# The opening of a spectral kernel: sine tables first with idle matmuls over the wait, and row statistics six rows ahead instead of eight

## The chip, the cores and the metric

The kernel runs on one core of a Trainium2 chip. The metric is the device time of one execution in microseconds, median over several executions. Every comparison below is with executions of the kernel before on the same chip in the same rounds.

## The reference, cut to what matters

The program computes a block with a spectral filter and a mixing layer over the sequence, and its gradients by `jax.vjp`.

```python
def _A_ref(x, w_r, w_i):              # x: 1 x 2048 x 448, bf16
    X = rfft2(x.astype(float32), axes=(-2, -1))
    X = X * (w_r + 1j * w_i)
    return irfft2(X, s=(2048, 448), axes=(-2, -1)).astype(bfloat16)

def _B_ref(x, w1, b1, w2, b2):
    h = layernorm(x)
    u = gelu(einsum("bsd,sf->bdf", h, w1) + b1)
    return (einsum("bdf,fs->bds", u, w2) + b2).transpose(0, 2, 1)

h  = x + _A_ref(layernorm(x), w_r, w_i)
h2 = h + _B_ref(layernorm(h), w1, b1, w2, b2)
# outputs: h2 and the gradients for grad_out with respect to x, w_r, w_i, w1, b1, w2, b2
# ... (inputs, random keys and helper names cut)
```

Only the start of it matters here. The 2048 rows of x are held as 16 "rows" of 128 partitions. Each needs its mean and deviation (the layer norm), and then enters the transform. Matrix multiplications of grad_out with w2 (a gradient of `_B_ref`) are independent of this, so the kernel uses them to fill TensorE between the row transforms.

## The kernel before

The Fourier transforms are matrix multiplications with sine tables that the kernel makes itself. For a row `t` of x, `scale_R` multiplies the table `Rm` by the row's reciprocal deviation (VectorE), `fold_prep` makes sums and differences of the two halves of two rows (VectorE), and `row_a` multiplies the two on TensorE. `row_b` follows four rows behind `row_a` with the second table, `csF`.

```python
def scale_R(t):
    v = Rs_ring.next()                                   # four buffers
    ve.tensor_scalar(out=v, in0=Rm[:], scalar1=rstd_x[:, t:t + 1], scalar2=None, op0=ALU.mult)
    return v

def newton_gp(v, y, sl):       # reciprocal deviations of two rows, ten dependent steps on GpSimd
    vi, yi = nt_i[:, 0, sl], y.bitcast(I32)
    a = nt_f[:, 0, sl]
    gp_.tensor_scalar(out=v, in0=v, scalar1=LN_EPS, scalar2=None, op0=ALU.add)
    gp_.tensor_scalar(out=yi, in0=v.bitcast(I32), scalar1=-0.5, scalar2=RSQRT_MAGIC, op0=ALU.mult, op1=ALU.add)
    for c0, c1 in RSQRT_STEPS:                           # two Newton steps
        gp_.tensor_tensor(out=a, in0=y, in1=y, op=ALU.mult)
        gp_.tensor_tensor(out=a, in0=a, in1=v, op=ALU.mult)
        gp_.tensor_scalar(out=a, in0=a, scalar1=c0, scalar2=c1, op0=ALU.mult, op1=ALU.add)
        gp_.tensor_tensor(out=y, in0=a, in1=y, op=ALU.mult)
```

The loop over the rows. `STATS[t]` lists the rows whose statistics VectorE takes in iteration `t`, `GROUPS[t]` the pair whose roots GpSimd then makes, and `fill(n)` issues n gradient matmuls.

```python
GROUPS = {0: (6, 8), 1: (8, 10), 3: (10, 12), 5: (12, 14), 7: (14, 16)}
STATS = {0: (6, 7), 1: (8, 9), **{t: (t + 8,) for t in range(2, 8)}}
# ...
for t in range(NT):                                      # NT = 16
    # ... (loads cut)
    if t + 1 < NT:
        row_a(t + 1, Rs.pop(t + 1))
    fill(FILL_A[t])
    if 1 <= t and t + 3 < NT:
        # ...
        Rs[t + 3] = scale_R(t + 3)
    row_b(t - 3)
    # ...
    if t % 2 and t < 12:
        fold_prep(xn, t // 2 + 2)
    for i in STATS.get(t, ()):
        ln_stats(xn, i, mvx)
    # ... (parts of the other sine tables cut)
    if t in GROUPS:
        a, b = GROUPS[t]
        newton_gp(mvx[:, a:b, 1], rstd_x[:, a:b], slice(a, b))
    # ...
    fill(FILL_B[t])
```

Copies of TensorE's results out of the tiles `ps_ff` and `ps_mm` may run on either VectorE or ScalarE.

Of the kernel before, what the change touches and what calls it, by code (L numbers as in the profile page):

```python
# [13 lines left out]
ALU = mybir.AluOpType  # L14
# [3 lines left out]
P = 128  # L18
# [83 lines left out]
class Ring:  # L102
# [7 lines left out]
    def next(self):  # L110
        v = self.views[self.i % len(self.views)]
        self.i += 1
        Ring.release(v)
        return v
# [8 lines left out]
def kernel(  # L123
# [20 lines left out]
    nc = tc.nc  # L144
# [3 lines left out]
    ve = Meter(nc.vector, load, 1)  # L148
# [13 lines left out]
    def cut(reg, off, *dims):  # L162
        n = int(np.prod(dims))
        v = reg[:, off:off + n]
        if len(dims) == 1:
            return v
        names = "abcd"[:len(dims)]
        return v.rearrange("p (" + " ".join(names) + ") -> p " + " ".join(names),
                           **{c: d for c, d in zip(names, dims)})
# [5 lines left out]
    def ps_ff(parts=P):  # L175
        return psum.tile([P, 512], F32, tag="ff", bufs=4, name="ps_ff")

    def ps_mm():
        return psum.tile([P, 512], F32, tag="mm", bufs=4, name="ps_mm")


    def evac(out, in_, scale=None):
        n = int(np.prod(in_.shape[1:]))
        if load[0] + sc.cost('copy', n, False) <= load[1] + ve.cost('tensor_copy', n, in_.dtype == BF16):
            if scale is None:
                sc.copy(out=out, in_=in_)
            else:
                sc.activation(out=out, in_=in_, func=ACT.Copy, scale=scale)
        elif scale is None:
            ve.tensor_copy(out=out, in_=in_)  # L190
        else:
            ve.tensor_scalar(out=out, in0=in_, scalar1=scale, scalar2=None, op0=ALU.mult)
# [24 lines left out]
    def mm(out, lhsT, rhs, start, stop):  # L217
        nc.tensor.matmul(out, lhsT=lhsT, rhs=rhs, start=start, stop=stop)  # L218
        clock[0] += int(np.prod(rhs.shape[1:])) / 2400.0
        run_due()  # L220
# [25 lines left out]
    csF = mem.tile([P, 2, 2, KW], BF16, name="csF")  # L246
    csI = mem.tile([P, 2, 2, D], BF16, name="csI")
    ident = mem.tile([P, P], BF16, name="ident")
# [6 lines left out]
    def col(n=1):  # L255
        i = _ci[0]
        _ci[0] += n
        assert _ci[0] <= 64
        return cols[:, i:i + n]

    xn = cut(rA, 0, NT, D)
# [26 lines left out]
    x_pt = A_x[0].rearrange("(p t) d -> p t d", t=NT)  # L288
# [3 lines left out]
    def load_w2T():  # L292
        j = w2T_ring.i
        if j == NFB:
            return
        wT = w2T_ring.next()
        nc.sync.dma_start_transpose(out=wT, in_=B_w2[j * P:(j + 1) * P, :].rearrange("f (t c) -> f t c", c=P))  # L297
        w2Ts.append(wT)
# [7 lines left out]
    def load_go(q):  # L306
        nc.sync.dma_start(out=go_tp[:, 4 * q:4 * q + 4, :], in_=go_tp_d[:, 4 * q:4 * q + 4, :])

    nc.sync.dma_start(out=xn[:, 0:2, :], in_=x_pt[:, 0:2, :])
    load_w2T()  # L310
    load_go(0)
    nc.sync.dma_start(out=xn[:, 2:4, :], in_=x_pt[:, 2:4, :])
    load_go(1)
    load_x(1)
    load_go(2)
# [13 lines left out]
    def ftmp(off, *dims):  # L329
        n = int(np.prod(dims))  # L330
        v = tf[:, off:off + n]
        if len(dims) == 1:
            return v
        names = "abcd"[:len(dims)]
        return v.rearrange("p (" + " ".join(names) + ") -> p " + " ".join(names),
                           **{c: d for c, d in zip(names, dims)})
# [11 lines left out]
    sc.activation(out=warm, in_=warm, func=ACT.Sin)  # L348
    nc.vector.memset(rAT[:, 0:512], 0.0)
    idle = ps_mm()  # L350
    for _ in range(12):
        nc.tensor.matmul(idle[:, 0:D], lhsT=rAT[:, 0:P], rhs=rAT[:, 0:D], start=True, stop=True)

    pcol = col()
# [4 lines left out]
    krow = ftmp(0, D)  # L359
# [169 lines left out]
    def gen_inv_cols(ch):  # L529
        e, en = col(), col()  # L530
        inv_cols[ch] = (e, en)
        gp_.memset(e, 2.0)
        if ch == 0:
            gp_.memset(e[0:1, :], 1.0)
        else:
            gp_.tensor_scalar(out=e, in0=pcolb, scalar1=112.0, scalar2=None, op0=ALU.is_equal)
            gp_.tensor_scalar(out=e, in0=e, scalar1=-1.0, scalar2=2.0, op0=ALU.mult, op1=ALU.add)
            gp_.memset(e[0:1, :], 0.0)
        gp_.tensor_scalar(out=en, in0=e, scalar1=-1.0, scalar2=None, op0=ALU.mult)
        gp_.tensor_scalar(out=halves[:, ch:ch + 1], in0=e, scalar1=-0.5, scalar2=1.5, op0=ALU.mult, op1=ALU.add)  # L540
# [82 lines left out]
    def scale_R(t):  # L623
        v = Rs_ring.next()
        ve.tensor_scalar(out=v, in0=Rm[:], scalar1=rstd_x[:, t:t + 1], scalar2=None, op0=ALU.mult)
        return v
# [5 lines left out]
    def fold_prep(src, t2):  # L632
        ft = fold_ring.next()
        s0 = 2 * t2
        fv = ft[:, 0:2 * D].rearrange("p (s w j) -> p s w j", s=2, w=2)
        a = src[:, s0:s0 + 2, 0:D // 2]
        r = src[:, s0:s0 + 2, D - 1:D // 2 - 1:-1]
        ve.tensor_tensor(out=fv[:, :, 0, :], in0=a, in1=r, op=ALU.add)
        ve.tensor_tensor(out=fv[:, :, 1, :], in0=a, in1=r, op=ALU.subtract)
        folds[t2] = ft  # L640
# [19 lines left out]
    def row_a(t, R):  # L660
        pa = ps_ff()
        ft = folds[t // 2]
        for k in range(4):
            o = DC * (4 * (t % 2) + k)
            mm(pa[:, k * P:(k + 1) * P], lhsT=ft[:, o:o + P], rhs=R, start=True, stop=True)
        if t % 4 == 0:
            blks[t // 4] = blk_ring.next()
        evac(out=blks[t // 4][:, :, :, t % 4, :], in_=pa[:].rearrange("p (a e b) -> p a e b", a=8, e=2))
# [125 lines left out]
    def fill(n):  # L794
        while n > 0 and pending:
            try:
                next(pending[0])
                n -= 1
                if row_ops:
                    row_ops.pop(0)()  # L800
            except StopIteration:
                pending.pop(0)
# [5 lines left out]
    def ln_stats(src, t, mv):  # L808
        ve.bn_stats(out=stats[:, t, :], in_=src[:, t, :])
        if t % 2:  # L810
            ve.bn_aggr(out=mv[:, t - 1, :], in_=stats[:, t - 1, :])
        if t % 2:
            ve.bn_aggr(out=mv[:, t, :], in_=stats[:, t, :])
# [36 lines left out]
    fwd_ops = gen_fwd_d()  # L850
    for fn in r_ops:
        fn()
    for fn in fwd_ops[:4]:
        fn()
    sc.activation(out=warm, in_=eps_x, func=ACT.Sqrt)
    base = ftmp(3072, 16, 16, 2)
    fix = ftmp(3584, 16)
# [9 lines left out]
        ln_stats(xn, t, mvx)  # L867
    sc.activation(out=rstd_x[:, 0:2], in_=mvx[:, 0:2, 1], func=ACT.Sqrt, bias=eps_x, scale=1.0)
    fold_prep(xn, 0)
    ve.reciprocal(out=rstd_x[:, 0:2], in_=rstd_x[:, 0:2])  # L870
    Rs = {t: scale_R(t) for t in range(2)}
    for t in range(2, 4):
        ln_stats(xn, t, mvx)
    sc.activation(out=rstd_x[:, 2:4], in_=mvx[:, 2:4, 1], func=ACT.Sqrt, bias=eps_x, scale=1.0)
    for fn in fwd_ops[4:6]:
        fn()
    ve.reciprocal(out=rstd_x[:, 2:4], in_=rstd_x[:, 2:4])
    for fn in fwd_ops[6:]:
        fn()
    nc.vector.memset(csF[:, 0, :, 0:1], 0.0)  # L880
    Rs.update({t: scale_R(t) for t in range(2, 4)})
    ve.tensor_scalar(out=ident[:], in0=krow[:, 0:P], scalar1=pcol, scalar2=None, op0=ALU.is_equal)
    gp_.memset(W_view_F[:, :, :, DF:KW], 0.0)
    w_loads = w_load()
    uv = gen_UV()
    gen_inv_cols(0)
    gen_inv_cols(1)
    row_a(0, Rs.pop(0))
    fold_prep(xn, 1)
    for t in (4, 5):  # L890
        ln_stats(xn, t, mvx)
    for fn in rstd_of(4, 6):
        fn()
    fill(6)
    turn_biases = load_biases()
    Meter.side, Meter.every, Meter.count = [], 1, 0
    GROUPS = {0: (6, 8), 1: (8, 10), 3: (10, 12), 5: (12, 14), 7: (14, 16)}
    STATS = {0: (6, 7), 1: (8, 9), **{t: (t + 8,) for t in range(2, 8)}}
    INV_S = {11: 0, 12: 1, 13: 2, 14: 3}
    for c in range(2):  # L900
        for e in range(2):
            sc.copy(out=Rp.rearrange("p (e a q b c) -> p c e a q b", e=2, c=2, q=8, a=2)[:, c, e],
                    in_=Rm[:, 64 * c + 32 * e:64 * c + 32 * e + 32].rearrange("p (q a b) -> p a q b", q=8, a=2))
    FILL_A = (3, 3, 3, 3, 3, 3, 3, 3, 3, 3, 3, 3, 3, 3, 3, 3)
    FILL_B = (3, 3, 3, 3, 3, 3, 3, 3, 3, 3, 3, 3, 3, 3, 3, 3)
    for t in range(NT):
        if t in (1, 3):
            load_w2T()
# [4 lines that stand above are left out]
# [8 lines left out]
# [4 lines that stand above are left out]
        for _ in range(3 if t > 0 else 0):  # L925
            if next(uv, None):
                break
# [3 lines that stand above are left out]
# [6 lines left out]
        if t == 2:  # L937
            gen_RT()
        fill(FILL_B[t])
    for i in range(2):  # L940
# [221 lines left out]
    for ch in range(2):  # L1162
        ve.tensor_scalar(out=csI[0:KC, :, ch, :], in0=csI[0:KC, :, ch, :], scalar1=halves[0:KC, ch:ch + 1], scalar2=None,
                         op0=ALU.mult)
# [84 lines left out]
    for t in range(NT):  # L1249
# [6 lines left out]
        pb, tmp, m1, m2, _ = ln_a(t, pdh[:, 0:D], rstd_h[:, t:t + 1], hln[:, t, :], (1.0 + LN_EPS) / D)  # L1256
# [195 lines left out]
```

## Time and profile before

| | kernel before |
|---|---|
| median of three runs | 356.7 us (356.2 to 357.64) |
| profiled run | 357.47 us, span 355.7 us |
| mean granted TensorE clock | 0.989 |
| PE busy | 341.0 us, 96% |
| row 5, row 8 and row 15 start on TensorE | 22.67, 28.09, 43.03 us |
| the second transform starts | 50.37 us |
| the inverse rows start | 86.23 us |

The fence is the timeline of TensorE in the kernel before (start, length, engine and line, operation, output<-inputs, count): the transform of row 15, the first matmuls of the second transform, and the first of the inverse row transforms. I use them to say by when a kernel is how far.

```profile
43.03 0.39 PE L218 MATMUL ps_ff<-rX,rS 128*128 128x128 bf16 x4
...
50.37 0.39 PE L218 MATMUL ps_ff<-permI,Vt 128*128 128x128 bf16 x4
...
86.23 0.83 PE L218 MATMUL ps_ff<-RTm,r 128*113 128x128 bf16 x12
```

The second is the timeline of VectorE in the same kernel, at the first multiplication with the spectral weights; it comes 11.36 us after the mark at 50.37.

```profile
61.73 1.17 DVE L82 TENSOR_TENSOR rS<-rX,rG 128x904 bf16<-128x904 bf16 x2
```

The first fence is the page's chain of work that ended last, by engine, and the second the list of VectorE's waits in the first 45 us (waiting line, releaser, us in total, times, longest). GpSimd has no share of the chain, and VectorE waits for it 0.2 us in all.

```profile
PE 73%; DVE 8%; ACT 7%; DMA 5%; issue 2%; SPq 2%; POOL 0%; DVEq 0%; ACTq 0%
```

```profile
DVE rX L82 <- POOL rstd_x L388: 0.2, 1, 0.2
```

### The profile page before, as it was taken

The page shows a single profiled execution, that of the slowest core. Times are in us where ns is not written, and L with a number is a line of the kernel's source. Part 1 is how long each engine was busy: PE and PEld are TensorE (multiplying, and loading weights), DVE is VectorE, ACT ScalarE, POOL GpSimd, SP SyncE. Part 2 cuts the span into 40 slices and gives each one's busy share as a digit, 9 for nine tenths or more (in the row PEclk, how much of TensorE's full clock was granted, in tenths as well). Part 3 has the DMA queues.
Part 4 walks back from the last instruction along what each step waited for, and adds up shares of the span by engine and source line. Part 5 has one row for each costly group of instructions (what it writes and reads, how often), then busy time and mean ns, then how long its engine had stood idle before and what let it go on. Part 6 is the DMA issues. An engine that isn't in the chain of part 4 may idle for free.

```text
span 355.7 us, 6447 instructions
## 1 busy us (share of the span) xinstructions
PE 341.0 (96%) x2133; PEld 183.8 (52%) x2133; DVE 254.5 (72%) x680; ACT 213.6 (60%) x457; POOL 69.1 (19%) x227
## 2 busy tenths in 40 slices
PE   5888999999999999999999999999999999999995
PEld 2345765555645555555555555544454544565542
DVE  5797638981884888776235888786595965499993
ACT  4549848965986545504222345566387866579872
POOL 8667100000221000001001111110000000067860
PEclk9699999999999999999999999999999999999999
DMA  8999969758999999977777999989966898799995
GB/s 209 272 186 211 235 172 184 161 163 284 280 292 357 299 350 237 251 218 222 183 186 150 190 213 189 216 151 300 292 180 194 231 232 248 228 203 265 245 282 218
DMA packets 147672, 81.62 MB, mean 229 GB/s; under 512 B 95480, under 2 KB 139768, under 8 KB 147384
## 3 DMA queue, kind: packets, MB, share of 16 engines
q1 hardware_dynamic: 147352, 80.83, 91.5%
q10 hardware_dynamic: 288, 0.39, 0.3%
q8 instruction: 16, 0.26, 0.3%
q14 instruction: 16, 0.13, 0.2%
HBM read 27.56 MB, written 23.89 MB: 145 GB/s over the span
## 4 chain that ended last, share of the span: by engine, by line
PE 73%; DVE 8%; ACT 7%; DMA 5%; issue 2%; SPq 2%; POOL 0%; DVEq 0%; ACTq 0%
PE ps_mm L218 61%; PE ps_ff L218 12%; DVE r L82 4%; DMA out_dram<-rG 2%; ACT rO L82 2%; DMA rB<-in_A_w_i_dram 2%; ACT rG L82 2%; DVE stats L82 2%; DMA rA<-in_A_x_dram 2%; SPq L297 1%; ACT Ut L82 1%; DVE rA L82 1%; DVE rS L82 1%; ACT rX L82 1%; ACT Vt L82 1%
## 5 line engine op out<-in xcount | busy, mean ns | idle before, releaser
L218 PEld LDWEIGHTS <-r 128*128 128x128 bf16 (+1 forms) x660 | 61.8, 104 | 49.6 <-issue 2.5
L218 PEld LDWEIGHTS <-rS 128*128 128x128 bf16 (+2 forms) x496 | 40.5, 98 | 38.3 <-issue 5.9
L218 PE MATMUL ps_mm<-rD,r 128*128 128x448 bf16 x224 | 44.5, 352 | 0.0
L82 ACT CAST rO<-ps_mm 128x512 bf16<-128x512 f32 (+1 forms) x66 | 35.2, 579 | 11.3 <-PE ps_mm L218 10.8
L218 PE MATMUL ps_mm<-rC,rE 128*128 128x448 bf16 x144 | 35.9, 370 | 3.6 <-DMA rC<-in_grad_out_dram 3.6
L218 PEld LDWEIGHTS <-rst 128*128 128x128 bf16 (+1 forms) x320 | 23.8, 97 | 29.0 <-issue 13.7
L218 PE MATMUL ps_mm<-r,rst 128*128 128x512 bf16 (+3 forms) x192 | 36.5, 353 | 0.0
L82 ACT CAST r<-ps_ff 128x452 bf16<-128x452 f32 x56 | 31.8, 575 | 7.6 <-PE ps_ff L218 7.4
L218 PE MATMUL ps_mm<-rB,r 128*128 128x448 bf16 x160 | 31.2, 352 | 0.1
L218 PE MATMUL ps_mm<-rG,rst 128*128 128x512 bf16 (+1 forms) x128 | 28.4, 380 | 0.0
L82 ACT ACTIVATE r<-ps_mm,rstd_h 128x448 bf16<-128x448 f32 x16 | 10.1, 633 | 26.8 <-PE ps_mm L218 26.8
L82 ACT ACTIVATE r<-rC 128x448 bf16<-128x448 bf16 x16 | 9.1, 571 | 26.7 <-DMA out_dram<-r 21.6
L82 DVE SCALAR_TENSOR_TENSOR r<-ps_mm,b2col,r 128x448 bf16<-128x448 f32 x16 | 10.9, 683 | 19.9 <-PE ps_mm L218 18.4
L82 ACT ACTIVATE rG<-rG 128x896 bf16<-128x896 bf16 x14 | 13.3, 950 | 14.9 <-DVE rG L82 14.7
L218 PEld LDWEIGHTS <-rO 128*128 128x128 bf16 (+1 forms) x165 | 15.6, 98 | 11.5 <-DMA rO<-in_B_w_dram 1.1
L218 PE MATMUL ps_mm<-rE,rS 128*128 128x448 bf16 x112 | 21.5, 352 | 0.0
L1182 POOL TENSOR_SCALAR lcol<-lcol 128x1 f32<-128x1 f32 x16 | 8.5, 530 | 64.7 <-ACT r L82 64.7
L218 PEld LDWEIGHTS <-rE 128*128 128x128 bf16 x148 | 14.4, 101 | 12.3 <-issue 5.6
L218 PE MATMUL ps_mm<-rC,rO 128*128 128x448 bf16 x80 | 19.1, 352 | 0.8 <-DMA rO<-in_B_w_dram 0.8
L1373 POOL TENSOR_SCALAR lcol<-lcol 128x1 f32<-128x1 f32 x16 | 4.7, 296 | 77.0 <-ACT r L82 76.9
L218 PE MATMUL ps_ff<-csI,rAT 113*128 113x224 bf16 (+1 forms) x108 | 19.0, 298 | 0.6 <-ACT rAT L82 0.4
L82 ACT CAST rG<-ps_mm 128x512 bf16<-128x512 f32 (+1 forms) x28 | 14.4, 550 | 8.1 <-PE ps_mm L218 8.0
(197 smaller groups left out, 661.0 us busy)
## 6 DMA issues: line engine op xcount, KB each, us to landing
out_dram<-rO SPq DMA_DIRECT2D x34, 256.0 KB
r<-in_B_w_dram SPq DMA_DIRECT2D x5, 1024.0 KB
r<-r SPq DMA_DIRECT2D x16, 226.0 KB
r<-r SPq DMA_DIRECT2D x32, 113.0 KB
rS<-in_B_w_dram SPq DMA_DIRECT2D x4, 896.0 KB
out_dram<-rG SPq DMA_DIRECT2D x10, 256.0 KB
rO<-in_B_w_dram SPq DMA_DIRECT2D x2, 1024.0 KB
w_d<-rG SPq DMA_DIRECT2D x1, 1808.0 KB
```

What stands on the lines that cost most here:

```text
L82: fn(**kw)
L218: nc.tensor.matmul(out, lhsT=lhsT, rhs=rhs, start=start, stop=stop)
L297: nc.sync.dma_start_transpose(out=wT, in_=B_w2[j * P:(j + 1) * P, :].rearrange("f (t c) -> f t c", c=P))
L1182: gp_.tensor_scalar(out=m1, in0=ms, scalar1=-1.0 / D, scalar2=None, op0=ALU.mult)
L1373: gp_.tensor_scalar(out=m1, in0=ms, scalar1=-2.0 / D, scalar2=None, op0=ALU.mult)
```

## The change

The intent is to shorten the opening. Rows 2 and 3 of x are loaded ahead of grad_out; the whole of the sine table `csF` is made before the first statistics, while VectorE would wait for x; more idle matmuls (on a zeroed tile, their result is not used) are to keep TensorE's clock up until grad_out lands. And the statistics are taken six rows ahead instead of eight, so that those of rows 8 and 9 no longer stand before rows 4 and 5. The fills are shifted accordingly.

```diff
     load_w2T()
+    nc.sync.dma_start(out=xn[:, 2:4, :], in_=x_pt[:, 2:4, :])
     load_go(0)
-    nc.sync.dma_start(out=xn[:, 2:4, :], in_=x_pt[:, 2:4, :])
 ...
-    for _ in range(12):
+    for _ in range(26):
         nc.tensor.matmul(idle[:, 0:D], lhsT=rAT[:, 0:P], rhs=rAT[:, 0:D], start=True, stop=True)
 ...
-    for fn in fwd_ops[:4]:
+    for fn in fwd_ops:
         fn()
+    nc.vector.memset(csF[:, 0, :, 0:1], 0.0)
 ... (the rest of fwd_ops, the memset and the identity tile leave their old places;
 ...  fold_prep(xn, 1) moves ahead of the scaling of rows 2 and 3)
+    fill(4)
     row_a(0, Rs.pop(0))
 ...
-    fill(6)
+    fill(0)
 ...
-    GROUPS = {0: (6, 8), 1: (8, 10), 3: (10, 12), 5: (12, 14), 7: (14, 16)}
-    STATS = {0: (6, 7), 1: (8, 9), **{t: (t + 8,) for t in range(2, 8)}}
+    GROUPS = {0: (6, 8), 3: (8, 10), 5: (10, 12), 7: (12, 14), 9: (14, 16)}
+    STATS = {0: (6, 7), **{t: (t + 6,) for t in range(2, 10)}}
 ...
-    FILL_A = (3, 3, 3, 3, 3, 3, 3, 3, 3, 3, 3, 3, 3, 3, 3, 3)
-    FILL_B = (3, 3, 3, 3, 3, 3, 3, 3, 3, 3, 3, 3, 3, 3, 3, 3)
+    FILL_A = (4, 4, 4, 3, 3, 4, 4, 4, 4, 4, 4, 3, 3, 3, 3, 3)
+    FILL_B = (0, 0, 0, 3, 3, 3, 3, 3, 3, 3, 3, 3, 3, 3, 3, 3)
```

More of the change, by code (lines that the diff above doesn't have):

```diff
@@ L869 @@
     fold_prep(xn, 0)
+    ve.tensor_scalar(out=ident[:], in0=krow[:, 0:P], scalar1=pcol, scalar2=None, op0=ALU.is_equal)
     ve.reciprocal(out=rstd_x[:, 0:2], in_=rstd_x[:, 0:2])
@@ L874 @@
     sc.activation(out=rstd_x[:, 2:4], in_=mvx[:, 2:4, 1], func=ACT.Sqrt, bias=eps_x, scale=1.0)
-    for fn in fwd_ops[4:6]:
-        fn()
+    fold_prep(xn, 1)
     ve.reciprocal(out=rstd_x[:, 2:4], in_=rstd_x[:, 2:4])
-    for fn in fwd_ops[6:]:
-        fn()
-    nc.vector.memset(csF[:, 0, :, 0:1], 0.0)
     Rs.update({t: scale_R(t) for t in range(2, 4)})
-    ve.tensor_scalar(out=ident[:], in0=krow[:, 0:P], scalar1=pcol, scalar2=None, op0=ALU.is_equal)
     gp_.memset(W_view_F[:, :, :, DF:KW], 0.0)
@@ L887 @@
     gen_inv_cols(1)
+    fill(4)
     row_a(0, Rs.pop(0))
-    fold_prep(xn, 1)
     for t in (4, 5):
```

## The prediction

> **What bounds the kernel now.** I read three things in this order: the page for the busiest engine, a table of windows for where TensorE is not full, and the timelines of the opening for what it waits for. The first fence is the page (engine, busy us, share of the span), the second the windows (stretch, its length, then each engine's busy time and count, granted clock, DMA share, GB/s).
>
> ```profile
> span 355.7 us, 6447 instructions
> PE 341.0 (96%) x2133; PEld 183.8 (52%) x2133; DVE 254.5 (72%) x680; ACT 213.6 (60%) x457; POOL 69.1 (19%) x227
> ```
>
> ```profile
> 1.20:31.00 29.80, 22.62 (x120) 11.32 (x121) 24.53 (x96) 17.00 (x36) 21.26 (x94) 0.89 1.07 225
> 31.00:100.00 69.00, 67.30 (x494) 42.85 (x492) 46.26 (x122) 53.01 (x112) 8.31 (x36) 1.00 0.91 216
> 100.00:356.00 256.00, 251.04 (x1524) 129.60 (x1522) 183.35 (x460) 143.12 (x312) 38.95 (x92) 1.00 0.91 234
> ```
>
> TensorE is full after 31 us. In the 29.8 us before, it is busy 22.6, of which 4.66 are the 12 idle matmuls and part runs at a granted clock of one half. Useful work there is small: 51 gradient matmuls at 0.19 us, nine row transforms of 0.22 and four of 0.39, some 13 us. So only the opening can give anything, and what it gives is how much earlier TensorE reaches the same amount of work. Its timeline (start, length, tile, count, idle before and releaser):
>
> ```profile
> 1.21 4.66 PE L352 MATMUL ps_mm<-rAT 128*128 128x448 bf16 x12 [1.21 <-DVE rAT L349]
> ...
> 9.22 0.92 PE L218 MATMUL ps_mm<-rC,rE 128*128 128x448 bf16 x4 [2.54 <-DMA rC<-in_grad_out_dram]
> ...
> 13.31 1.65 PE L218 MATMUL ps_mm<-rC,rE 128*128 128x448 bf16 x4 [0.27 <-DMA rC<-in_grad_out_dram]
> ...
> 19.97 0.64 PE L218 MATMUL ps_ff<-rX,rS 128*128 128x128 bf16 x4 [1.08 <-DVE rS L82]
> ...
> 30.67 0.57 PE L218 MATMUL ps_ff<-csF,rS 112*128 112x226 bf16 x4 [1.62 <-ACT rS L82]
> ```
>
> First TensorE waits for grad_out, then for row preparation on VectorE, last for a copy on ScalarE. VectorE is full from 14 to 34 us. Its timeline:
>
> ```profile
> 9.77 1.15 DVE L82 BATCH_NORM_STATS2 stats<-rA 128x6 f32<-128x448 bf16 x2 [3.57 <-DMA rA<-in_A_x_dram]
> 10.84 0.30 DVE L82 BATCH_NORM_AGGREGATE mvx<-stats 128x2 f32<-128x6 f32 x2
> 11.06 0.67 DVE L82 TENSOR_SCALAR r<-r 128x452 f32<-128x452 f32 x2
> ...
> 11.71 1.15 DVE L82 TENSOR_TENSOR r<-r 128x452 f32<-128x452 f32 x2
> 13.87 0.30 DVE L82 TENSOR_SCALAR rX<-Rm,rstd_x 128x128 bf16<-128x128 bf16 x1 [1.01 <-DVE r L82]
> ```
>
> It idles 3.57 us for rows 2 and 3 of x, then makes sine tables and waits 1.01 for their activation, before the rows go on. Those are the waits the change aims at. The last reading is GpSimd, which makes the reciprocal deviations for pairs of rows from 6 up:
>
> ```profile
> 19.56 0.44 POOL L382 TENSOR_SCALAR mvx<-mvx 128x2 f32<-128x2 f32 x1 [3.72 <-DVE mvx L82]
> ...
> 22.77 0.19 POOL L388 TENSOR_TENSOR rstd_x<-nt_f,rstd_x 128x2 f32<-128x2 f32 x1
> ```
>
> Ten dependent instructions, 3.4 us for the pair. Undisturbed steps come every 0.275 us, so 2.8 us is the floor.
>
> **What the Trainium skill says.** "TensorE: Matmul & The Clock Gate", Part 1, says the default clock is half, released after about 3.4 us of activity and taken away after an idle window. This trace agrees: the idle matmuls are 0.37 us apart, those at 9.22 us 0.19, those from 11 to 16.6 us 0.37 again (granted 0.50). "ScalarE: Activation LUTs", What ACT_TABLE_LOAD costs, gives about 1283 ns a load plus a drain; here each load is 1.28 us and needs no more. "DMA: Bandwidth & Descriptors", Anatomy of one DMA, gives about 2 us fixed: adding up the bytes moved, grad_out's first part should be through at about 7.0 us and is usable at 9.2. "GPSIMD Engine Reference", Key points, says GpSimd shares its SBUF interfaces with VectorE; steps of 0.4 to 0.6 us among those of 0.19 fit that.
>
> **The change part by part.** Instruction counts stay, but for 14 idle matmuls added; all else is order.
>
> *Loads.* Rows 2 and 3 of x (224 KB) go ahead of the first part of grad_out (448 KB). The two land at 9.2 and 9.75 now. Exchanged, x lands about 0.7 us before 9.2, near 8.5, and grad_out near 9.75. The later pieces have the same bytes ahead: second part of grad_out 10.96, third 13.31, rows 4 to 7 of x between them, near 12.2.
>
> *Tables first.* On VectorE 0.67 + 1.15 - 0.1 = 1.7 us move to where it idled. From 3.4 us they end at 5.1, both sine activations at 5.7 (0.53 each, one behind the other), the memset after them releases VectorE at 5.9, so rows 0 and 1 start there instead of 3.72. They took 2.5 us, with the identity tile 2.7: 8.6. That meets rows 2 and 3: statistics 1.4, fold 0.6, scaling 0.5, done at 11.1 instead of 15.04. Then VectorE must wait for x until 12.2. Rows 4 to 7, with the nine small Newton steps, took from 15.04 to 20.21; so row 4 can start at 17.4 instead of 19.97. The order of table loads is Sin, Sqrt, Sin as before; the third load (1.28) falls into ScalarE's 1.70 us wait.
>
> *Six ahead instead of eight.* Statistics of rows 8 and 9 leave the path of rows 4 and 5: 1.36 us off VectorE here, two single ones later. Row 5 can start at 18.6, 3.5 to 4 us earlier than now. But the pair 8, 9 now gets its deviations from GpSimd after iteration 3 for use in iteration 5 (today after 1 for 5), and so on up to 14, 15. This closes a loop: GpSimd 2.8 to 3.4, then on VectorE scaling, fold, statistics and aggregates of the next odd iteration, 1.55 (26.18 to 27.73 us in the trace), and two semaphores of about 0.1: 4.5 to 5.1 us for two rows. TensorE needs for two iterations 2 x (7 x 0.19 + 0.22 + 0.39) = 3.9. So the loop, not TensorE, sets the pace of rows 8 to 14.
>
> *Fill.* Up to row 4 TensorE has 16 gradient matmuls behind it instead of 24, up to the end of the rows 100 instead of 102. The missing ones are done later: 8 x 0.19 = 1.5 us owed at row 4, 2 x 0.19 = 0.38 at the end.
>
> *Idle matmuls.* Some 11 at 0.37, 15 at 0.19 end near 8.2 us, before grad_out is there. They cost nothing and shorten the gap before real work from 2.5 to 1.5 us. The clock may stay full, but TensorE waits for loads and VectorE until 17.4 either way, so a faster clock is worth nothing by itself.
>
> *The sum, step by step.* Row 4: 17.4 against 19.97, 2.6 less 1.5 owed, net 1.1. Row 5 at 19.2 (TensorE limited) against 22.67, 3.5 less 1.5, net 2.0. Row 8: statistics of 9 end at 21.9, GpSimd until 24.8, fold 25.7 against 28.09, less 1.1, net 1.3. The copy of row 7 on ScalarE (behind a table activation, five tile copies and five mask activations) ends near 27.9 where it now ends near 30.6: net 1.8 still. Then the loop takes over: with 4.6 us a turn the deviations of 10, 12, 14 come at 29.4, 34.0, 38.6, the fold for row 14 0.8 later, 39.4; row 15 at 41.3 against 43.03, 1.7 less 0.38, net 1.35. From there both run the same work with TensorE full, so 356.7 - 1.35 = 355.35. I take 355.3.
>
> **The rivals.** First, the loop is slower: 5.1 us a turn instead of 4.6 adds 4 x 0.5 = 2.0 us by row 14 and eats the gain, ending at 356 to 357.5. For it speaks the 3.4 us of a pair today; against it that VectorE then stands still and does not disturb GpSimd. Second, rows 8 to 11 of x arrive too late. Added-up bytes are through at 17.8 us, usable between 18.4 and 19.8, and statistics of row 8 now want them at 18.6; a wait up to 1.2 us would leave about 0.4 of the gain (356.3). Today they are wanted at 20.1, and the trace shows no wait. Third, everything VectorE and TensorE gain in the opening stays, GpSimd keeping up because the TensorE iterations are in fact longer: then the net 2.0 of row 5 and more holds, 354 to 354.6. Fourth, transfers take back the gain: at 61.8 us TensorE waits 0.8 for weights. That speaks for it; but the load was held until TensorE released its buffer at 49.8, and DMA is nearly empty from 45 to 49.5 us, so it moves with TensorE.
>
> **Range and chances.** The walk gives 1.35; the loop's length is worth -2.0 to +0.7, the late x up to -1.0, the two opening waits and the clock about 1 either way, and three runs of before spread from 356.2 to 357.64. Eight times in ten 353.4 to 357.3. A gain over 2% needs 7.1 us, more than the whole idle time outside the first load: 2%. A loss over 2% would need a new wait of over 8 us: 2%. Within 2%: 96%.
>
> **What would show it right or wrong.** Right: no third-of-the-opening idle of VectorE for rows 2 and 3 beyond some tenths, a new one near 11 to 12 us for rows 4 to 7; row 4 on TensorE near 17.4; VectorE's scaling of rows 8, 10, 12, 14 released by GpSimd, 5 to 7 us in all (0.2 today); the windows after 100 us unchanged. The memset waiting about 0.6 us for the sine activations near 5.2. Wrong: no waits on GpSimd (the loop is hidden), a wait of statistics for x at 18 to 20 us, TensorE slow past 18 us at half clock, or a longer wait for weights between 50 and 70 us.

## The result, and the profile after

The changed kernel took 358.4 us, median of four runs (358.27 to 358.6), against 356.81 us (356.2 to 357.64) for the kernel before in the same rounds: a ratio of 1.0043, 95% interval 1.0022 to 1.0065. A ratio is the mean time of one kernel's runs over the mean of the other's of the same rounds, so it is not quite the ratio of the medians. I had predicted a gain of 1.4 us, and the kernel lost 1.6; the time lies above my range.

The timeline of TensorE after the change, with the same columns (in brackets the idle time before, and what ended it):

```profile
1.21 7.07 PE L352 MATMUL ps_mm<-rAT 128*128 128x448 bf16 x26 [1.21 <-DVE rAT L349]
...
16.36 0.64 PE L218 MATMUL ps_ff<-rX,rS 128*128 128x128 bf16 x4 [1.59 <-DVE rS L82]
...
21.36 0.64 PE L218 MATMUL ps_ff<-rX,rS 128*128 128x128 bf16 x4 [1.07 <-DVE rS L82]
...
28.13 0.56 PE L218 MATMUL ps_ff<-csF,rS 112*128 112x226 bf16 x4 [0.91 <-ACT rS L82]
...
40.83 0.59 PE L218 MATMUL ps_ff<-rX,rS 128*128 128x128 bf16 x4 [0.92 <-ACT UTt L82]
...
43.01 0.39 PE L218 MATMUL ps_ff<-rX,rS 128*128 128x128 bf16 x4
...
50.35 0.39 PE L218 MATMUL ps_ff<-permI,Vt 128*128 128x128 bf16 x4
...
87.27 0.83 PE L218 MATMUL ps_ff<-RTm,r 128*113 128x128 bf16 x12
```

The opening did what it should: row 4 starts at 16.36 us, 3.61 earlier than before. Yet row 15 starts at 43.01, 0.02 earlier, and the inverse rows 1.04 us later than before. So the lead is lost between rows 4 and 15, and something more is lost between 50 and 87 us. Read row by row, from the same two timelines:

| row | 4 | 5 | 6 | 8 | 10 | 12 | 13 | 14 | 15 |
|---|---|---|---|---|---|---|---|---|---|
| before, start in us | 19.97 | 22.67 | 24.44 | 28.09 | 33.39 | 36.90 | 38.88 | 40.85 | 43.03 |
| after | 16.36 | 18.37 | 21.36 | 25.82 | 31.04 | 35.53 | 37.77 | 40.83 | 43.01 |
| lead | 3.61 | 4.30 | 3.08 | 2.27 | 2.35 | 1.37 | 1.11 | 0.02 | 0.02 |

The lead falls from row 6 on, but for a small rise at row 10, and is gone at row 14. Not all of the fall is loss. TensorE issues 72 gradient matmuls between rows 4 and 15, against 66 before: six of the eight owed at row 4 are done there, 6 x 0.19 = 1.14 us. Of the 3.59 us of lead lost from row 4 to row 15 the other 2.45 are added waits. At row 14 the bracket names ScalarE's copy into `UTt`, which ended at 40.78; the first half of row 14's fold ended at 40.73, so two waits end there within 0.05 us, and the trace alone can't say what the row would have done without the ring. The run with a shorter root, below, can: there row 14 starts at 38.00 without a wait.

The timeline of VectorE after the change shows where the waits come from. It lists the scaling of the first row of each pair, 6 to 14, and in between, from 30.11 on, what VectorE does in one turn; the last line is the first multiplication with the spectral weights.

```profile
20.75 0.26 DVE L82 TENSOR_SCALAR rX<-Rm,rstd_x 128x128 bf16<-128x128 bf16 x1 [1.75 <-POOL rstd_x L388]
...
25.21 0.25 DVE L82 TENSOR_SCALAR rX<-Rm,rstd_x 128x128 bf16<-128x128 bf16 x1 [1.91 <-POOL rstd_x L388]
...
30.11 0.26 DVE L82 TENSOR_SCALAR rX<-Rm,rstd_x 128x128 bf16<-128x128 bf16 x1 [2.01 <-POOL rstd_x L388]
30.28 0.69 DVE L82 TENSOR_TENSOR rS<-rA 128x448 bf16<-128x448 bf16 x2
30.89 0.62 DVE L82 BATCH_NORM_STATS2 stats<-rA 128x6 f32<-128x448 bf16 x1
31.42 0.30 DVE L82 BATCH_NORM_AGGREGATE mvx<-stats 128x2 f32<-128x6 f32 x2
...
34.92 0.25 DVE L82 TENSOR_SCALAR rX<-Rm,rstd_x 128x128 bf16<-128x128 bf16 x1 [1.05 <-POOL rstd_x L388]
...
40.12 0.32 DVE L82 TENSOR_SCALAR rX<-Rm,rstd_x 128x128 bf16<-128x128 bf16 x1 [2.58 <-POOL rstd_x L388]
...
62.38 1.17 DVE L82 TENSOR_TENSOR rS<-rX,rG 128x904 bf16<-128x904 bf16 x2
```

And GpSimd's timeline after the change: the end of the columns that it makes for the sine tables, the first root step for rows 6 and 7, then the first and last step for rows 10 and 11 and the first for rows 12 and 13.

```profile
17.51 0.19 POOL L407 TENSOR_TENSOR cols<-cols 128x1 f32<-128x1 f32 x1
17.78 0.23 POOL L382 TENSOR_SCALAR mvx<-mvx 128x2 f32<-128x2 f32 x1
...
26.91 0.21 POOL L382 TENSOR_SCALAR mvx<-mvx 128x2 f32<-128x2 f32 x1 [1.73 <-DVE mvx L82]
...
29.88 0.20 POOL L388 TENSOR_TENSOR rstd_x<-nt_f,rstd_x 128x2 f32<-128x2 f32 x1
...
31.81 0.28 POOL L382 TENSOR_SCALAR mvx<-mvx 128x2 f32<-128x2 f32 x1 [1.73 <-DVE mvx L82]
```

Each engine waits for the other, in a ring. GpSimd works from 26.91 to 30.08, 3.17 us, while VectorE stands still for 2.01 of them; then VectorE scales, folds, takes the statistics and the aggregates, 1.73 us with both hand-overs, while GpSimd stands still for the 1.73 in brackets. Together that is 4.90 us for two rows. TensorE needs 3.9 for them (rows 9 and 10, which wait for nothing, start 1.94 apart), so it is the ring that sets the pace.

The list of VectorE's waits in the first 45 us after the change, the answer to 0.2 us before, and the page's chain of the work that ended last, in which GpSimd now has 3% of the span where it had none:

```profile
DVE rX L82 <- POOL rstd_x L388: 9.3, 5, 2.6
```

```profile
PE 77%; ACT 6%; DVE 5%; DMA 3%; POOL 3%; issue 2%; SPq 2%; DVEq 0%; ACTq 0%
```

From the inverse rows on the two kernels take the same time: 355.7 - 86.23 = 269.47 us to the end before, 356.7 - 87.27 = 269.43 after. A line of the table by stretches (length, then busy time and count of each engine, granted clock, DMA share, GB/s) of the kernel before, then of the one after:

```profile
200.00:300.00 100.00, 99.30 (x628) 50.41 (x627) 74.65 (x178) 63.26 (x130) 6.97 (x13) 1.00 0.89 221
```

```profile
200.00:300.00 100.00, 99.30 (x632) 50.54 (x630) 75.24 (x179) 63.23 (x131) 6.99 (x13) 1.00 0.90 218
```

What stands between 50 and 87 us: from the second mark to the inverse rows the kernel before took 86.23 - 50.37 = 35.86 us, the one after 87.27 - 50.35 = 36.92. That stretch has no load of the opening in it, and it costs 1.06 us of its own.

### The profile page after: what moved, and what is told of

Same layout as the page of the kernel before. It is cut to its first block, busy times and chain, and to the rows that moved or that the text cites. A ratio compares the mean times of both kernels' runs of the same rounds, so it can differ in the third digit from the quotient of the medians.

```text
span 356.7 us, 6478 instructions
## 1 busy us (share of the span) xinstructions
PE 342.2 (96%) x2147; PEld 184.0 (52%) x2147; DVE 254.0 (71%) x678; ACT 215.5 (60%) x459; POOL 69.4 (19%) x227
## 4 chain that ended last, share of the span: by engine, by line
PE 77%; ACT 6%; DVE 5%; DMA 3%; POOL 3%; issue 2%; SPq 2%; DVEq 0%; ACTq 0%
PE ps_mm L218 65%; PE ps_ff L218 13%; ACT rO L82 2%; DMA rA<-in_A_x_dram 2%; DMA rB<-in_A_w_i_dram 2%; ACT rG L82 2%; DVE stats L82 1%; DVE rS L82 1%; SPq L297 1%; ACT rX L82 1%; DVE rA L82 1%; ACT Vt L82 1%; DVE r L82 1%; POOL nt_f L385 1%; POOL nt_f L386 1%
## 5 line engine op out<-in xcount | busy, mean ns | idle before, releaser
L218 PEld LDWEIGHTS <-rst 128*128 128x128 bf16 (+1 forms) x320 | 23.8, 97 | 29.0 <-issue 13.8
L218 PE MATMUL ps_mm<-rC,rE 128*128 128x448 bf16 x144 | 33.4, 352 | 1.9 <-DMA rC<-in_grad_out_dram 1.8
L82 ACT CAST rS<-ps_ff 128x512 bf16<-128x512 f32 x29 | 17.0, 588 | 3.8 <-PE ps_ff L218 3.8
```

What stands on the lines that cost most here:

```text
L82: fn(**kw)
L218: nc.tensor.matmul(out, lhsT=lhsT, rhs=rhs, start=start, stop=stop)
```

## The experiments

Theory A: the ring of VectorE and GpSimd, closed by the six-ahead, takes back the gain of the opening. The loss between 50 and 87 us is a second effect, with two parts: the two gradient matmuls that are issued later (100 instead of 102 in the rows, 2 x 0.19 = 0.38 us), and a later start of the multiplications with the spectral weights (62.38 - 50.35 = 12.03 us after the second mark instead of 11.36). Rivals: the tables-first order or the idle matmuls do harm; moved fills cost time as such; or the gain of the opening was never worth anything because a transfer ends last.

### New opening, eight ahead

The changed kernel with the two lines of before:

```diff
-    GROUPS = {0: (6, 8), 3: (8, 10), 5: (10, 12), 7: (12, 14), 9: (14, 16)}
-    STATS = {0: (6, 7), **{t: (t + 6,) for t in range(2, 10)}}
+    GROUPS = {0: (6, 8), 1: (8, 10), 3: (10, 12), 5: (12, 14), 7: (14, 16)}
+    STATS = {0: (6, 7), 1: (8, 9), **{t: (t + 8,) for t in range(2, 8)}}
```

> The changed kernel with row statistics eight ahead again (today's GROUPS and STATS), all of the new opening kept. Theory A, the GpSimd loop (statistics, ten GpSimd steps, scaling, fold, next statistics: 4.8 to 5.2 us for two rows) took back what the opening won: the loop opens, waits of VectorE for GpSimd fall from 9.3 us to under 2, row 15 on TensorE comes near 41 us instead of 43.0, and the time is 2 to 3 us under the changed kernel's 358.4, so 355.4 to 356.4. Rival B, the loss comes from the gradient matmuls put off and from the order of copies later, the loop being hidden: 358.0 to 358.8.

Measured: 356.81 us against 357.4, ratio 0.9976 (0.9952 to 1.0). VectorE waits for GpSimd 0.2 us as before the change; row 15 starts at 41.97, the inverse rows at 85.66. So the loss is gone once the ring is open, and a small gain may be left. It is smaller than I expected. The timeline of TensorE of this run shows what I had left out, at row 5:

```profile
16.76 0.64 PE L218 MATMUL ps_ff<-rX,rS 128*128 128x128 bf16 x4 [1.59 <-DVE rS L82]
...
20.80 0.40 PE L218 MATMUL ps_ff<-rX,rS 128*128 128x128 bf16 x4 [1.87 <-DVE rX L82]
```

With eight ahead, the statistics of rows 8 and 9 again stand before row 5, and TensorE waits 1.87 us. The change was right that they are in the way there.

### Old opening, six ahead

The same two lines the other way round, in the kernel before:

```diff
-    GROUPS = {0: (6, 8), 1: (8, 10), 3: (10, 12), 5: (12, 14), 7: (14, 16)}
-    STATS = {0: (6, 7), 1: (8, 9), **{t: (t + 8,) for t in range(2, 8)}}
+    GROUPS = {0: (6, 8), 3: (8, 10), 5: (10, 12), 7: (12, 14), 9: (14, 16)}
+    STATS = {0: (6, 7), **{t: (t + 6,) for t in range(2, 10)}}
```

> The kernel before with statistics six ahead alone. Theory A: from row 6 on the loop sets the pace also with the old opening, row 14 comes about 2 us later than today's 40.85, 358.5 to 359.5 us; waits of VectorE for GpSimd 6 us or more instead of 0.2. Rival B: statistics six ahead cost nothing by themselves, 356.4 to 357.2.

Measured: 359.27 us against 357.4, ratio 1.0048 (1.0023 to 1.0072). VectorE waits 7.4 us for GpSimd, five times; row 15 starts at 44.79, the inverse rows at 88.65. Six ahead by itself, without anything new in the opening, costs as much as the whole change did. The new order of tables and loads is not what does harm.

### One Newton step on GpSimd

The changed kernel with four of the ten dependent steps taken out. The result still passes the comparison with the reference.

```diff
-        for c0, c1 in RSQRT_STEPS:
+        for c0, c1 in RSQRT_STEPS[:1]:
```

> The changed kernel with one Newton step instead of two on GpSimd (four of ten instructions less for each pair of rows from 6 up; the deviations are then right to about a thousandth, which should pass). Theory A: a turn of the loop shortens by 4 x 0.275 = 1.1 us to some 3.8, about TensorE's own 3.9 for two rows, so the loop is hidden: VectorE's waits for GpSimd under 4 us, row 15 near 41.3, 356.2 to 357.0 us. Rival B: 358.0 to 358.8.

Measured: 356.01 us against 357.4, ratio 0.9964 (0.9933 to 0.9996), a little better than expected. The list of VectorE's waits:

```profile
DVE rX L82 <- POOL rstd_x L388: 2.6, 3, 0.9
```

The wait fell from 9.3 to 2.6 us, row 15 starts at 39.97 and the inverse rows at 84.19, both 3 us earlier than in the changed kernel. Four steps of 0.275 us are 1.1 us a turn, and 4.9 - 1.1 = 3.8 is just under TensorE's 3.9: the ring no longer sets the pace. (The two turns that its scalings show, at 19.86, 23.21 and 27.00, are 3.35 and 3.79.) The stretch from the second mark to the inverse rows is 36.88 us here, as long as in the changed kernel: the second loss doesn't come from the ring.

### The control: one Newton step in the kernel before

```diff
-        for c0, c1 in RSQRT_STEPS:
+        for c0, c1 in RSQRT_STEPS[:1]:
```

> The kernel before with one Newton step on GpSimd. If the step only helps by opening the loop: no change, 0.999 to 1.001 of the kernel before, rows from 4 to 15 in 23.1 us as now. If less GpSimd work helps anywhere[...]: 0.5 us or more faster.

Measured: 357.01 us against 357.23, ratio 0.9993 (0.997 to 1.0016). The rows 4 to 15 take 42.02 - 18.94 = 23.08 us, as in the profile of the kernel before (43.03 - 19.97 = 23.06). With eight ahead the same four steps are worth nothing that can be measured (0.3% at most, by the interval). So the saving above is not shorter work as such; it is the opening of the ring.

### A dose: two more GpSimd steps a pair

```diff
         vi, yi = nt_i[:, 0, sl], y.bitcast(I32)
         a = nt_f[:, 0, sl]
+        for _ in range(2):
+            gp_.tensor_scalar(out=a, in0=v, scalar1=1.0, scalar2=None, op0=ALU.mult)
```

> The changed kernel with two idle GpSimd instructions more at the head of each pair's reciprocal root (rows 6 to 15, five pairs). Theory A: each turn of the loop grows by 2 x 0.275 = 0.55 us, turns of 5.4 to 5.8 us instead of 4.8 to 5.2, and the five pairs add 2.2 to 2.8 us: row 14 on TensorE near 43.4 instead of 40.8, time 360.6 to 361.2. Rival B, the loop hidden: 358.0 to 358.8.

Measured in the changed kernel: 361.11 us, where the unaltered changed kernel on the same chip took 358.51, so 2.6 more. Against the kernel before (356.41) the ratio is 1.0128 (1.0112 to 1.0145). The scalings in VectorE's timeline, of rows 8 and 10:

```profile
26.25 0.25 DVE L82 TENSOR_SCALAR rX<-Rm,rstd_x 128x128 bf16<-128x128 bf16 x1 [2.50 <-POOL rstd_x L390]
...
31.70 0.25 DVE L82 TENSOR_SCALAR rX<-Rm,rstd_x 128x128 bf16<-128x128 bf16 x1 [2.57 <-POOL rstd_x L390]
```

(The line number is two higher than elsewhere because of the two added lines.) All five scalings stand at 21.18, 26.25, 31.70, 37.03 and 42.72, so each turn is 0.49 to 0.61 us longer than in the first profile. Two steps are 0.55 us a pair, five pairs 2.75 us, and 2.6 of them are in the time. A cost that passes through one to one lies on the path that sets the end.

### The same dose in the kernel before

> The kernel before with two idle GpSimd instructions more for each pair of rows (five pairs, 2.75 us of GpSimd in all). Theory A: statistics eight ahead leave GpSimd four iterations, there is no loop: under 0.4 us more, 356.4 to 356.8, where the same dose cost the changed kernel 2.6 us. Rival: GpSimd's own pace (3.4 us a pair against TensorE's 3.5 for two rows) already binds: 357.5 to 359.

The edit is the same. Measured: 358.37 us against 357.36, ratio 1.0028 (1.0004 to 1.0051). I had expected under 0.4 us more, and the time rose by 1.0; 358.37 even lies in the range of the rival, on a chip where the kernel before took 357.36. The rows 4 to 15 took 44.17 - 20.35 = 23.82 us instead of 23.06 to 23.09, 0.75 more, and VectorE waited 1.0 us for GpSimd. So eight ahead GpSimd also has little in hand: its pairs follow one another almost without a pause there too. But of 2.75 us added only about 0.75 reached the rows, and 1.0 the time (0.1 to 1.8 by the interval; the profiled run also waits 0.56 us right before the inverse rows), against 2.6 with six ahead. The contrast stands, though it is less sharp than I expected; the word "hidden" for GpSimd in the kernel before was too strong.

### Twelve idle matmuls again

```diff
-    for _ in range(26):
+    for _ in range(12):
```

> The changed kernel with 12 idle matmuls as before. Both theories: TensorE waits until 16.4 us for row 4 in any case, so the clock may be at half between 10 and 16 us and it costs nothing: 358.0 to 358.8. If the warm clock was worth something, over 358.9, with row 4 later than 16.4.

Measured: 358.35 us against 357.4, ratio 1.0021 (0.9997 to 1.0044), beside 358.4 for the unaltered changed kernel on another chip. Row 4 starts at 17.10 instead of 16.36, 0.7 later, row 6 at 21.37 (21.36) and row 15 at 43.03 (43.01). The granted clock from 10 to 16 us is 0.74, where it is 1.00 with 26 idle matmuls. The opening became slower and row 6 did not: the scaling of row 6 waits for GpSimd's first pair in both (20.76 and 20.75), and that takes up the difference. So in the traces the idle matmuls neither helped nor hurt; the unaltered changed kernel did not run on this chip, so the times say it less precisely.

### The changed kernel again, and its copies balanced as before

First the changed kernel unaltered on another chip.

> The changed kernel unaltered, as the measure for the others on this chip: a ratio of 1.003 to 1.006 to the kernel before.

Measured: 358.51 us against 356.41, ratio 1.0055 (1.0041 to 1.0069). Row 15 starts at 42.63; from the second mark at 49.97 to the inverse rows at 86.87 are 36.90 us. The loss repeats, and so does the long stretch.

The counters that share out copies are at other values when the spectral stage is built. This run sets them, 39.557 and 39.622 in the changed kernel, to those of the kernel before:

```diff
+    load[0], load[1] = 40.71072916666672, 40.59489583333336
     s2_stage(fwd_x, fwd_mult, ML_F, 3, 24, True)
```

> The changed kernel with one line more: ahead of the spectral stage the two load counters that share copies between ScalarE and VectorE are set to the values they have there in the kernel before (40.711, 40.595 instead of 39.557, 39.622). Theory C: of the 1.04 us that the changed kernel loses between 50 and 87 us, 0.38 are the two matmuls put off and 0.65 come from another share of copies, which starts VectorE's chain of multiplications at 62.4 instead of 61.7 us: here it starts near 61.7 and the time falls by 0.5 to 0.8 us, ratio about 0.0018 lower than the changed kernel's. Rival D: the chain is not what sets the end of that stage, or the share is no matter: no change (within 0.2 us).

Measured: 358.85 us, ratio 1.0068 (1.0053 to 1.0083): 0.34 slower than the changed kernel beside it, not faster. The multiplications still start 12.02 us after the second mark, and the stretch is 37.37 us. The expectation failed: the counters alone are not the cause of the second loss.

### The fills of the rows as many as before

```diff
-    FILL_A = (4, 4, 4, 3, 3, 4, 4, 4, 4, 4, 4, 3, 3, 3, 3, 3)
+    FILL_A = (4, 4, 4, 3, 3, 4, 4, 4, 4, 4, 4, 3, 3, 4, 4, 3)
```

> The changed kernel with the two put-off gradient matmuls done inside the rows, one more in iterations 13 and 14 each (TensorE waits 0.92 us ahead of row 14, so one of them fits into a wait). If only their own time counts: 0.38 us less, 358.1 against 358.5, the stretch from the end of the rows to the inverse rows (36.92 us, 35.86 in the kernel before) 0.38 shorter. Theory C2: the two matmuls also shift the accumulator copies against the spectral stage, and the other 0.65 us go with them: 1.0 us less, 357.4 to 357.6, multiplications of VectorE starting 11.4 us after the end of the rows instead of 12.0.

Measured: 358.39 us against 356.36, ratio 1.0053 (1.0041 to 1.0065), no gain. The stretch became 0.37 us shorter (36.53) and the rows 0.38 longer, as two matmuls of 0.19 must do when TensorE has no room for them where they are put. I had hoped that they would fall into the ring's idle time, but the two places that I chose, iterations 13 and 14, lie behind it. The 0.38 us owed are a debt that moves; they are not a loss to be saved this way.

Both edits together, fills and counters:

> The changed kernel with the two put-off matmuls back inside the rows and the load counters as in the kernel before, so that copies in the spectral stage have the kernel before's order and share. If these make the lost 0.65 us: the stretch from the end of the rows to the inverse rows is 36.0 to 36.1 us as in best1 (35.86 in the kernel before, 36.92 in the changed one), the rows end 0.38 later for the two matmuls, and the time is 0.4 to 0.5 us below the changed kernel, ratio 1.004. If not, ratio 1.005 to 1.006.

Measured: 358.02 us against 357.36, ratio 1.0022 (1.0001 to 1.0043), in two groups, four runs at 357.83 to 358.05 and two at 358.79 and 358.84. The profile fell in the slower group, with a wait of 1.06 us before the inverse rows. Without that wait its stretch is 36.24 us, and the multiplications start 11.32 us after the second mark, as in the kernel before. So with the fills and the counters both as before, the later start of the multiplications is gone; with one of the two it is not (12.02 with the counters, 11.79 with the fills). That supports the second effect, about 0.65 us from the share and the order of the copies, but two groups of runs are not a clean proof. Two runs from above narrow it. With eight ahead in the new opening the multiplications start 11.04 us after the second mark (60.35 - 49.31), though fills and counters were left alone; with six ahead in the old opening 11.40. So the late start comes with the six-ahead and the moved fills together, not with either alone. Which copy makes it was not shown.

### The parts of the opening alone

Each in the kernel before with eight ahead: the tables first (with its order of folds and the identity tile), and the loads exchanged.

```diff
-    for fn in fwd_ops[:4]:
+    for fn in fwd_ops:
         fn()
+    nc.vector.memset(csF[:, 0, :, 0:1], 0.0)
 ... (and the later parts of fwd_ops taken out, fold_prep(xn, 1) in their place)
```

> The kernel before with only the tables first (and fold and identity placed as in the change); load order, 12 idle matmuls, fills and eight ahead as before. Theory A: this is where the opening's gain is: row 4 about 2 us earlier than 19.97, then limited by rows 4 to 7 of x; with the loop open most of it stays: 354.8 to 356.0 against 356.6, ratio 0.995 to 0.998. If later waits (weights, copies on ScalarE) take it back, the ratio is over 0.999.

```diff
+    nc.sync.dma_start(out=xn[:, 2:4, :], in_=x_pt[:, 2:4, :])
     load_go(0)
-    nc.sync.dma_start(out=xn[:, 2:4, :], in_=x_pt[:, 2:4, :])
```

> The kernel before with only rows 2 and 3 of x loaded ahead of grad_out's first part: they land 0.7 to 1.2 us earlier and the whole VectorE chain moves up by that: row 4 at 18.8 to 19.3 instead of 19.97, 355.6 to 356.2 against 356.6. If TensorE's later start with grad_out costs as much, no change.

Measured against 356.36: tables first 355.84, ratio 0.9989 (0.9972 to 1.0007); loads 355.89, ratio 0.9987 (0.9973 to 1.0002). In the traces row 15 starts at 40.73 and 40.48, more than 2 us earlier than in the profile of the kernel before, but the medians differ by 0.5 us only, within the interval. In the first, a wait of 0.62 us before the inverse rows took some of it back. Neither part does harm, which is what the question was; how much each gains could not be settled. One reason is that my profiles of the kernel before are all of its slower executions, which the next two runs show.

### The kernel before, profiled twice more

No edit; single executions, whose state is unknown.

> The kernel before, unaltered, for another profile. If its fast runs at 356 to 356.5 us differ from the profiled one at 357.47 in the opening: row 15 at 42 us instead of 43.0 and the inverse rows at 85.2 instead of 86.2. If the difference lies later, the rows are as in the first profile.

> As before_p1: a second sample of where runs of the kernel before differ.

Measured: 357.81 and 358.2 us, where eleven executions on that chip had a median of 357.36 and went from 355.96 to 358.1. In the first, row 15 and the second mark are at 42.32 and 49.65, 0.7 earlier than in the first profile, and then, in TensorE's timeline:

```profile
86.77 0.85 PE L218 MATMUL ps_ff<-RTm,r 128*113 128x128 bf16 x12 [1.14 <-ACT rD L82]
```

The copy named as the releaser had ended at 86.20, so the wait of 1.14 us was for something else; by its place it may be the last of the transfers that reorder the data for the inverse rows, which the profile doesn't show. In the second, TensorE's wait for w2 (0.8 us at 61.8 us in the first profile) was 1.6. So the kernel before loses up to about 1 us in some executions between 50 and 87 us, once for certain to a transfer, and every profile of it unaltered was taken in a run above its median. The comparison of the two traces therefore understates the loss: 357.47 to 358.6 is 1.13 us, and the medians differ by 1.6 to 2.1.

### Versions that try to win

The changed kernel with one Newton step, the fills and the counters:

```diff
-        for c0, c1 in RSQRT_STEPS:
+        for c0, c1 in RSQRT_STEPS[:1]:
-    FILL_A = (4, 4, 4, 3, 3, 4, 4, 4, 4, 4, 4, 3, 3, 3, 3, 3)
+    FILL_A = (4, 4, 4, 3, 3, 4, 4, 4, 4, 4, 4, 3, 3, 4, 4, 3)
+    load[0], load[1] = 40.71072916666672, 40.59489583333336
```

> The changed kernel with one Newton step on GpSimd, the two put-off matmuls done inside the rows (one more in iterations 13 and 14), and the load counters as in the kernel before. If the three losses add up: 356.0 - 0.38 - 0.65, about 355.0 us, a ratio of 0.993 to 0.996 to the kernel before. If the later stage is held by transfers, no better than one Newton step alone.

Measured: 354.87 us against 356.41, ratio 0.9956 (0.9942 to 0.997), and 3.64 us below the changed kernel on the same chip. Its timeline of TensorE:

```profile
39.95 0.39 PE L218 MATMUL ps_ff<-rX,rS 128*128 128x128 bf16 x4
...
83.55 0.83 PE L218 MATMUL ps_ff<-RTm,r 128*113 128x128 bf16 x12
```

Row 15 starts 2.7 us earlier than in the changed kernel beside it, and the stretch is 36.07 us instead of 36.90 (35.86 before the change): the first loss is gone and the second nearly. This version is faster than both kernels, clear of the noise but by 0.4% only against the kernel before, and it pays with a root that is right to about a thousandth.

The same with six more gradient matmuls in iteration 7, to spend earlier what TensorE might have of idle time:

```diff
-    FILL_A = (4, 4, 4, 3, 3, 4, 4, 4, 4, 4, 4, 3, 3, 4, 4, 3)
+    FILL_A = (4, 4, 4, 3, 3, 4, 4, 10, 4, 4, 4, 3, 3, 4, 4, 3)
```

> The changed kernel with one Newton step, the load counters as before, and six gradient matmuls more in iteration 7, where TensorE waits 1.5 us for the copy of row 7 on ScalarE (then fewer at the end of the spectral stage). If that wait is filled and the stage's end needs no padding: 1.1 us less than best1's 354.9, some 353.8. If the weights aren't there yet or the stage's end then waits: 354.5 to 355.

Measured: 357.46 us against 356.36, ratio 1.002 (1.0004 to 1.0036). A miss. The list of TensorE's waits names the reason:

```profile
PE ps_mm L218 <- DMA rO<-in_B_w_dram: 2.7, 1, 2.7
```

The weights for the added matmuls had not landed, and TensorE stood 2.7 us before them.

Last, the better version with eight ahead again:

```diff
-    GROUPS = {0: (6, 8), 3: (8, 10), 5: (10, 12), 7: (12, 14), 9: (14, 16)}
-    STATS = {0: (6, 7), **{t: (t + 6,) for t in range(2, 10)}}
+    GROUPS = {0: (6, 8), 1: (8, 10), 3: (10, 12), 5: (12, 14), 7: (14, 16)}
+    STATS = {0: (6, 7), 1: (8, 9), **{t: (t + 8,) for t in range(2, 8)}}
```

> best1 (new opening, one Newton step, the two matmuls back, the load counters) with statistics eight ahead. Rows 8 and 9 then stand in front of row 5 again (1.36 us of VectorE), as in new_eight where TensorE waited 1.9 us there: 0.3 to 1.0 us slower than best1, ratio 0.996 to 0.999. If six ahead is worth nothing: as best1, 0.994 to 0.996.

Measured: 356.57 us against 357.23, ratio 0.9989 (0.9966 to 1.0012), row 15 at 42.79 in a profile of its slowest execution (358.04). Against 0.9956 with six ahead: once the ring is shorter than TensorE's two iterations, six ahead looks worth about 0.3%, as the change intended. The two were run on different chips and their intervals touch, so the size is uncertain.

## Why the prediction was wrong

**The opening was right.** Row 4 was put at 17.4 us and came at 16.36; VectorE no longer waits for rows 2 and 3 of x, and only 0.41 us, until 11.34, for rows 4 to 7, which I had put at 12.2: most of the 1.0 us by which row 4 was early; it idles 0.66 us before 5.80, for the sines, where I had said about 0.6; the idle matmuls end at 8.28 (8.2); row 8 came at 25.82 (25.7), the matmul that waits for the copy of row 7 at 28.13 (27.9). The clock stays full (granted 1.00 from 8 to 16 us), and it is worth nothing, as argued. Grad_out's first part was put too late, 9.75 us; TensorE started on it at 8.51. The stretches after 100 us are unchanged.

**The step that failed first: "with 4.6 us a turn".** The mechanism of the ring was in the prediction; its size was not. The turns from scaling to scaling are 4.46, 4.90, 4.81 and 5.20 us; the three that I counted after row 8 are the last three, 14.91 us instead of 13.8. VectorE's half was right: 1.55 us and two hand-overs of 0.1 make 1.75, and GpSimd stands still for 1.73 in every turn. GpSimd's half was mis-sized: 4.6 leaves it 2.85 us, near the low end of my 2.8 to 3.4, and the pairs took 2.73, 3.17, 3.08 and 3.47. The last is longest because two instructions of another task, 0.29 and 0.28 us, were issued between its steps.

On top, the scaling for row 8 came at 25.21, 0.4 after the 24.8 that I had written. That began with rows 6 and 7: GpSimd was still making columns until 17.7 us, although the statistics it needed were done at 15.9, and before the change those columns were done at 15.83. The new order had held them back: GpSimd stood still for 2.52 us until 6.03, for a memset that VectorE now does after the sine tables; before, it went on at 3.61. I had not looked at what moving the tables does to GpSimd.

So the deviations of row 14 came at 40.12 instead of 38.6: 0.4 from the late start and 1.1 from the turns. The rest follows from these: row 14 at 40.83 (39.4), row 15 at 43.01 (41.3). The term of 1.7 us of gain measured 0.02.

I had seen this as the first rival, "5.1 us a turn ... eats the gain", and gave it too little weight; the last three turns are 4.97 us on average. The argument against it, that VectorE stands still and therefore doesn't disturb GpSimd, held only in part. The pairs are shorter than before the change (four of them took 3.39 to 3.53 us there), but VectorE used the rest of each turn to make other sine tables. A step of 0.66 us instead of 0.20, at 27.48 in GpSimd's timeline, lies beside such table work (27.41 to 28.10), and one of 0.47, at 32.76, too (32.74 to 33.17). That the one delays the other was not tested.

**The step that failed second: "From there both run the same work with TensorE full".** It is the same work by count, but not in the same order. The stretch to the inverse rows took 1.06 us more: 0.38 for the two matmuls that I had counted, and 0.67 for a later start of the multiplications on VectorE, which I had not. That I read nothing of how the counters share out copies later is the gap in the working. The cause is supported by the fills-and-counters run and by the better version, and refuted for the counters alone; beyond that it stays open.

**The sum.** 355.35 + 1.7 for the ring + 0.7 for the second stretch gives 357.7; measured were 358.4. The 0.6 to 0.7 left lie within what the profiles of the kernel before leave open: they were all taken in runs above its median, so the marks of its typical run are not known to better than about 1 us. One profile shows a fast execution, that of the control (one Newton step in the kernel before, which changed no time), at 356.45 us: there row 15 starts at 42.02 and the inverse rows at 85.22. Against it the two profiles of the changed kernel (42.63 and 43.01, then 86.87 and 87.27) are 0.6 to 1.0 us late at row 15 and 1.65 to 2.05 at the inverse rows, as much as the medians differ. So in a typical pair of runs row 15 is probably not early by 0.02 but late; one such profile does not settle by how much. That the ring is the main part is shown: the two lines exchanged in each kernel, the shortened root and the dose all moved the time in the direction that it says.

**The other rivals.** The late rows of x (second rival) showed no wait. That everything gained would stay (third) was refuted. That transfers take it back (fourth) was not what happened: the wait for weights is gone from the profile after. And the chance of a change over 2% was rightly small.

**The signs.** None of the four signs that I had listed for being wrong came, and those for being right did, the waits for GpSimd among them. What differed was their size: 7.55 us before rows 8, 10, 12 and 14, and 1.75 before row 6, which I had not foreseen, 9.3 in all where I had written 5 to 7. The kinds of wait alone could not tell a ring that costs a part of the gain from one that costs all of it.

## What to carry to other kernels

A lead in a software pipeline is not only a delay at the start: shortening it from eight rows to six closed a ring of two engines that each wait for the other, and such a ring costs the sum of both latencies, however idle each engine looks. Before shortening a lead, add up the ring, every dependent step with the disturbance that it really suffers, and compare it with the pace of the bounding engine. A gain at the start that is smaller than the ring's spread times its number of turns (here some 0.5 us by three or four, against 1.35) is not yet a gain. And where the programmer's own scheduler shares out work by counters, a change in one stage must be read in the next stage too.

## What the Trainium skill lacked or had wrong

- "GPSIMD Engine Reference", 3.1 Elementwise, gives the time of a `tensor_tensor` at 2048 elements (4497 ns) and names two software dispatch hops, but no time for a small instruction. Here the tiny ones of 128x2 elements last 0.19 to 0.20 us and follow one another, dependent, every 0.275 us; some take 0.4 to 0.66. Ten of them took 2.73 to 3.17 us after the change, and 3.47 with two others between them.
- "ScalarE: Activation LUTs", What ACT_TABLE_LOAD costs, adds about 1380 ns of drain to each load. The two traces don't show it: all five loads of each kernel take 1.28 us on average, and the next instruction starts at most 0.02 us after each; after the change the load at 18.55 us ends at 19.83 and the next activation starts at 19.85.
- No page gives the time of a hand-over between GpSimd and VectorE. Here it adds little to the ring, 0.03 and 0.09 us (the ends of GpSimd's steps are rough in these profiles): GpSimd's last step ends at 30.08 and VectorE's scaling starts at 30.11; VectorE's aggregates end at 31.72 and GpSimd starts at 31.81.
